# A second MoE with its last weight splits inside an expert's own first matmul and two narrower tiles, and an attention whose natural rows and one routing step are placed elsewhere

## Chip, core, metric

One core of a Trainium2 chip. The metric is the device time of one execution in microseconds; lower is better. The core has five engines that the text names: TensorE (PE in the profile, PEld for its weight loads), VectorE (DVE), ScalarE (ACT), GpSimd (POOL) and SyncE (SP, which here only issues DMAs).

## What is computed

Three stages run one after the other on 1536 tokens (2 batches of 768) of width 512 (8 heads of 64).

```python
# attention: a query sees the keys of its own cluster only
q_assign = argmax(q_n @ c_n.T); k_assign = argmax(k_n @ c_n.T)      # 16 clusters per head
scores = where(q_assign == k_assign, q @ k.T / 8, -1e9)
x = softmax(scores) @ v                                             # (1536, 512)
# first MoE: tokens with x @ w_skip > 0 go through one of 8 experts
x[sel] = x[sel] + gate * (relu(x[sel] @ w1[e]) @ w2[e])             # w1: 512x1024, w2: 1024x512
# second MoE, capacity 384 per expert
out = gate * (relu(x @ w1b[e]) @ w2b[e])                            # 0 for tokens over capacity
```

## The kernel before

**Attention.** Heads are worked in pairs g = 0 to 7. A hand-written schedule places calls at units u; a pair takes 12 units (2 heads x 6 key blocks). In each unit a score tile (`score_mm`, L290) goes through the exponential on ScalarE (L298), is rounded (L299) and its remainder taken on GpSimd (L301), and three units later it multiplies v (`pv`). Between them stand the preparation of the pair three ahead (`prep_T` psT, `prep_as`, `prep_oh`, `prep_mk`, and `stack_q`, whose DMAs fill AA and BB), the row maxima (`mpass`, L272) and the end of the pair before: `fin_den` and `fin_nat(g, 0)`, `fin_nat(g, 1)`. `fin_nat` makes half of a pair's rows in token order with three matmuls into psN, scales them into `xn` on VectorE, adds the routing logits into `lg` (L372), and in its second half issues two DMAs that store `xn` to `xa` and `xb`. All these take one PSUM tile at a time from a pool of six (`ps_w`). The orders of TensorE, ScalarE, GpSimd and SP are as written; VectorE's is the planner's in this stage.

**Routing in attention.** `early(lg)` is a generator whose steps run as hooks at units u0 + i (u0 = 58). It routes the first batch's tokens and finds the two experts to start with; the step at u0 + 6 picks these two in turn (L750 to L760), with its short-lived values in a PSUM tile (`scratch`).

**The second MoE.** `run` ends in a loop over places t = 1 to 7, where the experts stand sorted by their count, `caps` being the tokens that each place holds: 128, 256, 320, 256, 256, 256, 256, 128. The loop is written out in the order that every engine follows, VectorE too. An expert's first matmul (`l1`, L1432 to L1434) has 8 rows f of 4 x 3 matmuls, each with 128 columns of weights and caps[t] columns of x; a PSUM tile (two of them) holds two rows, or one where caps[t] is 320. ScalarE (L1437) and VectorE (L1438) then make ReLU and its remainder: `hh` and `hl`, and for the columns past 256 `hA`. The second matmul (`l2`, L1122 to L1124) takes 24 matmuls of 512 columns for each 128 tokens. Both use three products of rounded parts, and so each 512 KB piece of weights is split once (`split`): cast on ScalarE (L1036), remainder on VectorE (L1037). Pieces 0 to 3 are of the first matrix, 4 to 7 of the second; nine pairs of buffers (`spl`) hold them. The last place (t = 7 = Z) runs its first matmul unsplit. `nsplit` splits pieces of the next expert: piece 0 after the first quarter of `l1`, pieces 1 to 4 after `l1`, pieces 5 to 7 after `l2`. The pieces land in two sets of buffers that alternate, so `load(n + 2, i)` waits until piece i of expert n has been split.

Of the kernel before, what the change touches and what calls it, by code (L numbers as in the profile page):

```python
# [14 lines left out]
ALU = mybir.AluOpType  # L15
AX = mybir.AxisListType
# [6 lines left out]
def attention(ctx, tc, q, k, v, centroids, wcat, lgacc, xa, xb, idw, hooks, bind):  # L23
# [4 lines left out]
    C = S // 128  # L28
    HP = H // 2
    NP = B * HP  # L30
# [347 lines left out]
    def at(u, fn, *a):  # L378
        sched.setdefault(u, []).append((fn, a))
# [29 lines left out]
    for g in range(NP):  # L409
        u = 2 * C * g  # L410
        if g > 1:
            at(u + -32, load, g)
            at(u + -32, load_V, g)
        if g == 0:
            at(-20, load_V, 0)
            at(-20, load_V, 1)
            for x in ((prep_T, 0, 0), (cen_T,), (prep_H, 0, 0), (prep_L, 0, 0), (prep_T, 0, 1), (prep_H, 0, 1), (prep_L, 0, 1),
                      (prep_T, 0, 2), (prep_H, 0, 2), (prep_as, 0, 0), (prep_as, 0, 1), (stack_q, 0, 0, 0), (stack_q, 0, 1, 0),
                      (next, su), (prep_oh, 0, ((0, 1),)), (prep_as, 0, 2), (warm, 5), (prep_mk0, 0), (prep_oh, 0, ((1, 2),)),
                      (prep_L, 0, 2), (warm, 4), (prep_mk0, 1), (warm, 1), (stack_q, 0, 0, 1), (stack_q, 0, 1, 1),  # L420
                      (prep_V, 0)):
                at(-20, *x)
        else:
            w = (-10, -7, -7) if g == 1 else [u + x for x in (-21, -20, -18)]
            for i in range(3):
                at(w[i], prep_T, g, i)
            if g == 1:
                for i, (l, h) in enumerate(zip((-6, -5, -3), (-6, -5, -4))):
                    at(h, prep_H, g, i)
                    at(l, prep_L, g, i)  # L430
            w = (-5, -4, -3) if g == 1 else [u + x for x in (-19, -17, -16)]
            for i in range(3):
                at(w[i], prep_as, g, i)
            w = -1 if g == 1 else u + -14
            at(w, prep_oh, g)
            w = 3 if g == 1 else u + -12
            at(w, prep_mk, g)
            for h in range(2):
                x = 1 if g == 1 else w + 0
                at(x, stack_q, g, h, 0)  # L440
                at(x, stack_q, g, h, 1)
                at(w, stack_mk, g, h)
        if g:
            at(u + -10 if g > 1 else -2, prep_V, g)
        at(u + 2 * C + -3, fin_w, g)
        at(u + 2 * C + 4, fin_den, g)
        at(u + 2 * C + 4, fin_nat, g, 0)
        at(u + 2 * C + 5, fin_nat, g, 1)
    for u in sorted(set(sched) | set(hooks)):
        with ExitStack() as man:  # L450
            if u < 7:
# [8 lines left out]
class Moe:  # L460
    def __init__(self, ctx, tc, xa, xb, out, w1a, w2a, w1b, w2b, wg2, ident, landA, J=12):
# [13 lines left out]
        con, E, C = self.con, self.E, self.C  # L475
# [24 lines left out]
        self.tri = tri  # L500
        self.thr = {}
        self.c0 = {1: 128, 2: 256}
        self.caps = [128, 256, 320] + [256] * (E - 4) + [128]
        self.slots = [(p, i) for i in range(3) for p in range(E) if self.caps[p] > 128 * i]
        self.nov = (N_TOK - 128) // 128
        for m in (1, 2):
# [185 lines left out]
    def early(self, lg):  # L692
        nc, V, sm, E, C = self.nc, self.nc.vector, self.at, self.E, self.C
# [6 lines left out]
        def scratch(*ns):  # L700
            ps, o, out = self.ps(), 0, []
            for n in ns:
                out.append(ps[:, o:o + n])
                o += n
            return out

        by = lambda t, e: t.rearrange("p (j e) -> p j e", e=e)
# [16 lines left out]
        g, r = scratch(C, C)  # L724
# [9 lines left out]
        key = sm.tile([128, E], F32, name="key")  # L734
# [8 lines left out]
        ab = sm.tile([128, 2, E], F32, name="ab")  # L743
        es = sm.tile([128, 2], F32, name="pes")
        lh = sm.tile([128, 2], F32, name="lohi")
        mk = sm.tile([128, 2, 2], F32, name="pmk")
        abp, t, esp = scratch(2 * E, E, 2)
        abp = by(abp, E)
        for i in range(2):
            V.tensor_reduce(out=mk[:, i, 0:1], in_=key, axis=AX.X, op=ALU.max)  # L750
            V.tensor_scalar(out=abp[:, i], in0=key, scalar1=mk[:, i, 0:1], scalar2=None, op0=ALU.is_equal)
            V.tensor_tensor(out=t, in0=abp[:, i], in1=self.w8[:, 0, :], op=ALU.mult)
            V.tensor_reduce(out=mk[:, i, 1:2], in_=t, axis=AX.X, op=ALU.add)
            V.tensor_scalar(out=esp[:, i:i + 1], in0=mk[:, i, 1:2], scalar1=-1.0, scalar2=float(E), op0=ALU.mult, op1=ALU.add)
            if i == 0:
                V.scalar_tensor_tensor(out=key, in0=abp[:, 0], scalar=-65536.0, in1=key, op0=ALU.mult, op1=ALU.add)
        V.tensor_reduce(out=lh[:, 0:1], in_=esp.unsqueeze(1), axis=AX.X, op=ALU.min)
        V.tensor_reduce(out=lh[:, 1:2], in_=esp.unsqueeze(1), axis=AX.X, op=ALU.max)
        V.tensor_copy(es, esp)
        V.tensor_copy(ab, abp)  # L760
        yield
        self.eA = self.expert(es[:, 0:1], "dA", sm)
        self.eB = self.expert(es[:, 1:2], "dB", sm)
# [14 lines left out]
        abp, iap, kp = scratch(2 * E, 2 * C, C)  # L778
        abp, iap = by(abp, E), by(iap, C)
# [27 lines left out]
        inf, t, S = self.ids(self.spread(R0, rhs0, C), 2, self.rt, "e")  # L807
# [222 lines left out]
    def split(self, t):  # L1030
        nc = self.nc
        shp = [128, self.F]
        h = self.spl.tile(shp, F32R, name="wh")
        l = self.spl.tile(shp, F32R, name="wl")
        src = t if len(t.shape) == 2 else t.rearrange("p f d -> p (f d)")
        nc.scalar.copy(h, src)  # L1036
        nc.vector.tensor_tensor(out=l, in0=src, in1=h.bitcast(F32), op=ALU.subtract)  # L1037
        return h, l
# [314 lines left out]
    def run(self, lg, cap):  # L1353
# [7 lines left out]
        def load(n, i, t=None):  # L1361
            if n >= N:
                return
            if n >= n1:
                p = n - n1
                if p > 1 and p not in r2n:
                    r2n[p] = self.reg(self.namei2[:, p:p + 1])
                w = self.load(2, r2n.get(p, p), n, i, t)
            else:
                if n not in rL:  # L1370
                    rL[n] = self.reg(self.namei[:, n - 2:n - 1])
                w = self.load(1, rL[n], n, i, t)
            L[n, i] = w
# [13 lines left out]
        def put_splits(n, t, ks, i0):  # L1387
            for i, k in enumerate(ks):
                at(*divmod(17 * t + k, 17), lambda i=i0 + i: split(n, i))
# [144 lines left out]
        at(T, 7, lambda: self.fin2(S[n1], psU))  # L1534
        at(T, 4, lambda: xts(1, 0))
        at(T, 7, lambda: xts(1, 1))
        put_splits(n1 + 1, n1 + 1, (1, 2, 4, 5, 8, 9, 11, 13), 0)
        psS = play(T, self.l1_steps(sS["xt"], L1, hh, None) + self.l2n_steps(hh, W2(n1)))
        loads(n1 + 2, 4, 8)()
        self.fin2(sS, psS)  # L1540
# [1 line left out]
        Z = E - 1  # L1542
        for t in range(1, E):
            n = n1 + t
            for i in range(4, 8):
                load(n + 2, i)

            def nsplit(*ii):
                for i in ii:
                    if t + 1 < Z or t + 1 == Z and i >= 4:  # L1550
                        split(n + 1, i)

            hh, hl = self.new_h(256)
            if self.caps[t] > 256:
                h3 = self.rt.tile([128, 2, 8, 64], F32R, name="hA")
                self.h3 = h3[:, 0], h3[:, 1]
            nxt = sub(t + 1) if t < Z else []
            for s in nxt:
                self.gather(2, s)
            for k in range(4 if t < Z else 2):  # L1560
                if t < Z:
                    l1(t, k, hh, hl)
                else:
                    self.l1_native(sub(t)[0]["xt"], [L[n, i] for i in range(4)], k, hh[:, :, 0:128], hl[:, :, 0:128])
                if k == 0:
                    nsplit(0)
            nsplit(1, 2, 3, 4)
            for i in range(4):
                load(n + 2, i)
            pre = [lambda i=i: xts(t + 1, i) for i in range(len(nxt))] if t + 1 < Z else \  # L1570
                [lambda: self.xt_native(nxt[0])] if nxt else []
            for i, s in enumerate(sub(t)):
                ps = self.ps2()
                w = width(t, i)
                W2 = [SP[n, j] for j in range(4, 8)]
                self.l2(hh, hl, W2, range(0, 4), ps, i, w)
                if pre and (i or len(pre) == 3):
                    pre.pop(0)()
                self.l2(hh, hl, W2, range(4, 8), ps, i, w)
                self.fin2(s, ps, w)  # L1580
                if pre and i == 0:
                    pre.pop(0)()
            nsplit(5, 6, 7)
        self.overflow(2, [L[N - 1, i] for i in range(8)])
@with_exitstack
def tile_kernel(ctx, tc, q, k, v, centroids, moe_w_skip, moe_w_gate, moe_w1, moe_w2,
# [6 lines left out]
    with tc.manual_schedule(engines={ET.PE, ET.SP, ET.Pool, ET.Activation}):  # L1593
# [37 lines left out]
        for _k, _v in ((3, [early]), (u0 + 17, [moe.startA, moe.gatherAB]), (u1 + -14, [moe.xtA]), (u1 - 18, [swap]), (u1 + 2, [lambda: moe.l1A(0)]), (u1 + 6, [lambda: moe.l1A(1)])):  # L1631
            hooks.setdefault(_k, []).extend(_v)
        er = moe.early(lg)
        for i in (0, 1, 2, 4, 6, 8, 9, 11, 12, 13, 15):
            hooks.setdefault(u0 + i, []).append(lambda: next(er))
        for i in range(8):
            hooks.setdefault(u0 + 18 + i, []).append(lambda i=i: moe.loadA(i))
# [39 lines left out]
```

## Time and profile before

| | |
|---|---|
| Median of 3 runs | 659.49 us (656.88 to 660.16) |
| The profiled execution | 660.25 us; its span, first to last instruction, 658.4 us |
| Mean granted TensorE clock | 0.991 |
| Busy: PE, PEld, DVE, ACT, POOL | 623.5, 536.0, 404.0, 370.6, 259.7 us |

Busy time is the union of an engine's instructions. Matmuls are pipelined, so the distance between the starts of two of them, not the duration of one, tells their pace. Attention fills the span to about 300 us, the first MoE to about 467, the second to the end.

### The profile page before, as it was taken

To read this page: it belongs to the slowest core of one execution; us is meant where nothing else is said; L and a number is where in the kernel's file an instruction comes from. 1 tells how busy PE (TensorE), PEld (TensorE's weight loads), DVE (VectorE), ACT (ScalarE), POOL (GpSimd) and SP (SyncE) were. 2 spreads that over 40 slices of the span, in tenths; PEclk is the share of its full clock that TensorE was granted. 3 is DMA by queue.
4 is the path that set the end of the run, shared out by engine and by line. 5 is a ranking of instruction groups with operands and counts; after the bars stand their busy time and mean duration, and the time that the engine had idled before them with its cause. 6 is when DMAs were issued, how large, how long until landed. Compare 5 with 4: busy or idle time off the path is not lost. (4 is left out here: it accounts for less than half of the span.)

```text
span 658.4 us, 11633 instructions
## 1 busy us (share of the span) xinstructions
PE 623.5 (95%) x4104; PEld 536.0 (81%) x4104; DVE 404.0 (61%) x1003; ACT 370.6 (56%) x624; POOL 259.7 (39%) x197
## 2 busy tenths in 40 slices
PE   7889999999998999999999999999999899999994
PEld 6668888888877887879588999888778879888983
DVE  5958676767678785515777676655855536547431
ACT  4777787878778688872243443421355336455340
POOL 7665767777756578830120111100131112312110
PEclk9999999999999999999999999999999899999998
DMA  7964848484844549451478788882196616457100
GB/s 225 217 135 108 193 94 187 98 187 102 184 106 97 121 97 318 177 144 50 127 260 325 274 324 297 290 303 97 53 369 258 256 64 253 170 203 271 40 19 18
DMA packets 77104, 117.02 MB, mean 178 GB/s; under 512 B 27313, under 2 KB 42673, under 8 KB 77040
## 3 DMA queue, kind: packets, MB, share of 16 engines
q1 hardware_dynamic: 72752, 103.98, 52.7%
q0 software_dynamic: 4288, 12.24, 5.4%
q8 instruction: 34, 0.56, 0.3%
q14 instruction: 30, 0.25, 0.1%
HBM read 83.45 MB, written 12.98 MB: 146 GB/s over the span
## 5 line engine op out<-in xcount | busy, mean ns | idle before, releaser
L301 POOL TENSOR_TENSOR Pl<-P,Ph 128x768 fp32r<-128x768 f32 x93 | 170.3, 1840 | 69.3 <-ACT Ph L299 32.2
L1037 DVE TENSOR_TENSOR wl<-l,wh 128x1024 fp32r<-128x1024 f32 x84 | 99.9, 1221 | 57.1 <-ACT wh L1036 57.1
L272 DVE TENSOR_REDUCE m<-psx 128x1 f32<-128x384 f32 x192 | 98.0, 550 | 33.8 <-PE psx L271 32.9
L290 PE MATMUL pss<-BB,AA 128*128 128x384 f32 (+1 forms) x384 | 88.4, 352 | 9.4 <-DVE lg L372 3.6
L298 ACT ACTIVATE P<-pss 128x384 f32<-128x384 f32 x192 | 83.8, 489 | 23.1 <-PE pss L290 18.6
L1036 ACT CAST wh<-l 128x1024 fp32r<-128x1024 f32 x84 | 84.4, 1045 | 0.0
L299 ACT CAST Ph<-P 128x768 fp32r<-128x768 f32 x96 | 80.1, 835 | 4.2 <-PE pso L318 1.2
L290 PEld LDWEIGHTS pss<-BB,AA 128*128 128x128 f32 (+1 forms) x384 | 65.8, 190 | 16.0 <-ACT P L298 4.2
L1059 PE MATMUL psl<-xt,l 128*128 128x128 f32 x640 | 78.0, 277 | 0.4 <-ACT xt L1210 0.4
L1059 PEld LDWEIGHTS psl<-xt,l 128*128 128x128 f32 x640 | 74.8, 192 | 1.7 <-ACT xt L1210 0.5
L1156 POOL DMA_INDIRECT out_dram<-y,vsi x15 | 15.1, 1005 | 134.5 <-ACT y L1155 115.3
L316 PE MATMUL pso<-Ph,VA 128*65 128x384 f32 x192 | 65.7, 342 | 0.7 <-ACT DN L333 0.7
L318 PE MATMUL pso<-Ph,VL 128*64 128x384 f32 x192 | 65.9, 343 | 0.0
L320 PE MATMUL pso<-Pl,VA 128*65 128x384 f32 x192 | 65.6, 342 | 0.2 <-DVE Pl L301 0.2
L1432 PE MATMUL psl<-xh,wh 128*128 128x256 f32 (+1 forms) x192 | 55.7, 290 | 4.5 <-DVE hA L1438 2.7
L271 PE MATMUL psx<-AA,BB 128*128 128x384 f32 x192 | 51.6, 352 | 4.0 <-DVE m L272 1.5
L1433 PE MATMUL psl<-xl,wh 128*128 128x256 f32 (+1 forms) x192 | 54.9, 286 | 0.0
L1434 PE MATMUL psl<-xh,wl 128*128 128x256 f32 (+1 forms) x192 | 54.8, 285 | 0.0
L1148 POOL DMA_INDIRECT xb<-x,fsi x8 | 8.1, 1016 | 102.6 <-DVE x L1147 88.1
L271 PEld LDWEIGHTS psx<-AA,BB 128*128 128x128 f32 x192 | 34.1, 189 | 11.3 <-ACT P L298 5.0
L1122 PE MATMUL psl<-wh,hh 128*128 128x512 f32 x104 | 41.9, 403 | 0.0
L1432 PEld LDWEIGHTS psl<-xh,wh 128*128 128x128 f32 x192 | 36.6, 191 | 5.8 <-issue 3.0
(408 smaller groups left out, 1175.0 us busy)
## 6 DMA issues: line engine op xcount, KB each, us to landing
l<-in_moe_w_dram SPq DMA_DIRECT2D x128, 512.0 KB, 5.3
AA<-qkH SPq DMA_DIRECT2D x14, 384.0 KB, 4.9
vn<-in_v_dram SPq DMA_DIRECT2D x8, 384.0 KB
BB<-qkL SPq DMA_DIRECT2D x16, 192.0 KB, 3.4
xa<-xn SPq DMA_DIRECT2D x8, 384.0 KB
xb<-xn SPq DMA_DIRECT2D x8, 384.0 KB, 5.0
AA<-qkL SPq DMA_DIRECT2D x31, 96.0 KB, 4.1
BB<-qkH SPq DMA_DIRECT2D x31, 96.0 KB, 3.6
```

What stands on the lines that cost most here:

```text
L271: nc.tensor.matmul(ps, BB[:, 0, qc * 128:(qc + 1) * 128], AA[:, 0, f * HF:(f + 1) * HF], start=True, stop=True)
L272: nc.vector.tensor_reduce(out=hs[h]["m2"][:, qc, f:f + 1], in_=ps, axis=AX.X, op=ALU.max)
L290: nc.tensor.matmul(ps, AA[0:K, t, kc * 128:(kc + 1) * 128], BB[0:K, t, sl], start=(t == 0), stop=(t == 1))
L298: nc.scalar.activation(out=P[:, f * HF:(f + 1) * HF], in_=ps, func=AF.Exp, scale=1.0 / 8.0)
L299: nc.scalar.copy(Ph, P)
L301: eng.tensor_tensor(out=Pl, in0=P, in1=Ph.bitcast(F32), op=ALU.subtract)
L316: nc.tensor.matmul(o[0:D + 1, :], va, Ph[:, sl], start=(kc == 0), stop=False)
L318: nc.tensor.matmul(o[0:D, :], vl, Ph[:, sl], start=False, stop=False)
L1036: nc.scalar.copy(h, src)
L1037: nc.vector.tensor_tensor(out=l, in0=src, in1=h.bitcast(F32), op=ALU.subtract)
L1059: nc.tensor.matmul(st[k][:, q, :], L1[c][:, f * 128:(f + 1) * 128], xt[:, c, :], start=(c == 0), stop=(c == 3))
L1432: nc.tensor.matmul(ps[:, q, :], wh[:, fs], xh[:, c, 0:W], start=(c == 0), stop=False)
```

## The change

In attention, `fin_nat(g, 0)` and `fin_nat(g, 1)` of all pairs but the last stand one and two units later. The routing step that picks two experts becomes two steps with a PSUM tile each, one per expert, and the steps behind it come one unit later (the sixth stands at u0 + 6, the new seventh at u0 + 7). In the second MoE, places 5 and 6 hold 224 and 192 tokens instead of 256. Pieces 5 to 7 of an expert's weights are split inside its own `l1`, one after each of the first three quarters; pieces 0 to 4 of the next expert all follow `l1`; for the last place pieces 5 to 7 do too. Before the loop five pieces of the first expert are split instead of eight. `load(n + 2, 4..7)` moves from the loop's head to behind `load(n + 2, 0..3)`.

```diff
-        at(u + 2 * C + 4, fin_nat, g, 0)
-        at(u + 2 * C + 5, fin_nat, g, 1)
+        at(u + 2 * C + (5 if g < NP - 1 else 4), fin_nat, g, 0)
+        at(u + 2 * C + (7 if g < NP - 1 else 5), fin_nat, g, 1)
...
-        self.caps = [128, 256, 320] + [256] * (E - 4) + [128]
+        self.caps = [128, 256, 320] + [256] * (E - 6) + [224, 192, 128]
...
-        abp, t, esp = scratch(2 * E, E, 2)
-        abp = by(abp, E)
         for i in range(2):
+            abp, t, esp = scratch(E, E, 1)
             V.tensor_reduce(out=mk[:, i, 0:1], in_=key, axis=AX.X, op=ALU.max)
...
-        V.tensor_reduce(out=lh[:, 0:1], in_=esp.unsqueeze(1), axis=AX.X, op=ALU.min)
-        V.tensor_reduce(out=lh[:, 1:2], in_=esp.unsqueeze(1), axis=AX.X, op=ALU.max)
-        V.tensor_copy(es, esp)
-        V.tensor_copy(ab, abp)
+            V.tensor_copy(es[:, i:i + 1], esp)
+            V.tensor_copy(ab[:, i], abp)
+            if i == 0:
+                yield
+        V.tensor_reduce(out=lh[:, 0:1], in_=es.unsqueeze(1), axis=AX.X, op=ALU.min)
+        V.tensor_reduce(out=lh[:, 1:2], in_=es.unsqueeze(1), axis=AX.X, op=ALU.max)
...
-        put_splits(n1 + 1, n1 + 1, (1, 2, 4, 5, 8, 9, 11, 13), 0)
+        put_splits(n1 + 1, n1 + 1, (1, 2, 5, 9, 12), 0)
...
-            for i in range(4, 8):
-                load(n + 2, i)
...
-                if k == 0:
-                    nsplit(0)
-            nsplit(1, 2, 3, 4)
+                if t < Z and k < 3:
+                    split(n, 5 + k)
+            nsplit(0, 1, 2, 3, 4)
+            if t + 1 == Z:
+                nsplit(5, 6, 7)
             for i in range(4):
                 load(n + 2, i)
+            for i in range(4, 8):
+                load(n + 2, i)
...
-            nsplit(5, 6, 7)
...
-        for i in (0, 1, 2, 4, 6, 8, 9, 11, 12, 13, 15):
+        for i in (0, 1, 2, 4, 6, 7, 9, 10, 12, 13, 14, 16):
             hooks.setdefault(u0 + i, []).append(lambda: next(er))
```

## Rows read from the trace of the kernel before

**Rows 1.** The page, part 1: busy us, share of the span, instructions.

```profile
PE 623.5 (95%) x4104; PEld 536.0 (81%) x4104; DVE 404.0 (61%) x1003; ACT 370.6 (56%) x624; POOL 259.7 (39%) x197
```

**Rows 2.** Waits of PE over the span: us in total, times, longest.

```profile
PE pss L290 <- DVE lg L372: 3.6, 4, 1.2
...
PE psl L1432 <- DVE hA L1438: 2.7, 1, 2.7
PE psl L1432 <- DVE hl L1438: 1.7, 4, 0.4
...
PE pss L290 <- DVE key L756: 1.2, 1, 1.2
...
PE pss L290 <- DVE ab L760: 0.9, 1, 0.9
```

**Rows 3.** Timeline, place t = 2: start, duration (us), engine, instruction, idle time before.

```profile
508.01 2.93 ACT L1036 CAST wh<-l 128x1024 fp32r<-128x1024 f32 x3
...
513.06 0.38 ACT L1437 ACTIVATE hh<-psl 128x256 fp32r<-128x256 f32 x1
...
509.08 3.50 DVE L1037 TENSOR_TENSOR wl<-l,wh 128x1024 fp32r<-128x1024 f32 x3 [3.64 <-ACT wh L1036]
512.49 0.42 DVE L1438 SCALAR_TENSOR_TENSOR hl<-psl,hh 128x256 fp32r<-128x256 f32 x1
...
514.19 0.23 DVE L1438 SCALAR_TENSOR_TENSOR hA<-psl,hA 128x64 fp32r<-128x64 f32 x1 [0.29 <-ACT hA L1437]
...
513.57 0.61 PE L1432 MATMUL psl<-xh,wh 128*128 128x320 f32 x1 [2.72 <-DVE hA L1438]
```

**Rows 4.** Windows at half clock: length, busy of PE to POOL, clock, DMA share, GB/s.

```profile
513.20:516.60 3.40, 3.03 (x11) 3.06 (x12) 2.10 (x4) 1.40 (x3) 0.26 (x1) 0.50 0.98 344
...
212.80:216.20 3.40, 3.40 (x14) 3.04 (x13) 2.50 (x6) 0.90 (x2) 1.82 (x1) 0.50 0.01 2
```

**Rows 5.** Timeline of PE where place t = 3 waits.

```profile
548.40 0.28 PE L1434 MATMUL psl<-xh,wl 128*128 128x256 f32 x1
549.11 0.39 PE L1432 MATMUL psl<-xh,wh 128*128 128x256 f32 x1 [0.43 <-DVE hl L1438]
```

**Rows 6.** The pace of matmuls: the chain that ended last, and timelines.

```profile
451.01 0.90 PE psq L1177 x8
...
599.97 0.28 PE L1432 MATMUL psl<-xh,wh 128*128 128x256 f32 x1
...
601.67 0.28 PE L1432 MATMUL psl<-xh,wh 128*128 128x256 f32 x1
...
480.32 0.19 PEld L1128 LDWEIGHTS psl<-l,hh 128*128 128x128 f32 x1 [0.24 <-issue]
...
482.46 0.19 PEld L1128 LDWEIGHTS psl<-l,hh 128*128 128x128 f32 x1 [0.24 <-issue]
```

**Rows 7.** One group by form from 480 us: busy, mean ns of one.

```profile
L1438 DVE SCALAR_TENSOR_TENSOR hl<-psl,hh 128x512 fp32r<-128x512 f32 x20 | 13.8, 689 | 22.7 <-ACT hh L1437 22.1 <-issue 0.6
```

**Rows 8.** Timeline of ACT, place t = 2, two rows f one after the other.

```profile
518.73 0.38 ACT L1437 ACTIVATE hh<-psl 128x256 fp32r<-128x256 f32 x1 [0.66 <-PE psl L1434]
...
520.51 0.38 ACT L1437 ACTIVATE hh<-psl 128x256 fp32r<-128x256 f32 x1 [0.68 <-PE psl L1434]
```

**Rows 9.** Timeline of DVE, second matmul of place t = 5.

```profile
603.78 4.63 DVE L1037 TENSOR_TENSOR wl<-l,wh 128x1024 fp32r<-128x1024 f32 x4 [0.24 <-ACT wh L1036]
...
611.96 0.69 DVE L1420 TENSOR_TENSOR xl<-psxT,xh 128x512 fp32r<-128x512 f32 x1 [2.32 <-ACT xh L1419]
```

**Rows 10.** Timeline of PE and ACT, end of the second pair in attention.

```profile
101.31 0.60 PE L147 MATMUL psT<-idw,qkn 128*128 128x128 f32 x4
...
107.26 0.58 ACT L149 CAST qkH<-psT 128x512 fp32r<-128x512 f32 x1 [2.15 <-DMA BB<-qkH]
107.75 0.88 ACT L298 ACTIVATE P<-pss 128x384 f32<-128x384 f32 x2
...
108.99 0.59 PE L290 MATMUL pss<-BB,AA 128*128 128x384 f32 x2 [1.17 <-DVE lg L372]
```

More of the change, by code (lines that the diff above doesn't have):

```diff
@@ L746, in early @@
         mk = sm.tile([128, 2, 2], F32, name="pmk")
-        abp, t, esp = scratch(2 * E, E, 2)
-        abp = by(abp, E)
         for i in range(2):
+            abp, t, esp = scratch(E, E, 1)
             V.tensor_reduce(out=mk[:, i, 0:1], in_=key, axis=AX.X, op=ALU.max)
-            V.tensor_scalar(out=abp[:, i], in0=key, scalar1=mk[:, i, 0:1], scalar2=None, op0=ALU.is_equal)
-            V.tensor_tensor(out=t, in0=abp[:, i], in1=self.w8[:, 0, :], op=ALU.mult)
+            V.tensor_scalar(out=abp, in0=key, scalar1=mk[:, i, 0:1], scalar2=None, op0=ALU.is_equal)
+            V.tensor_tensor(out=t, in0=abp, in1=self.w8[:, 0, :], op=ALU.mult)
             V.tensor_reduce(out=mk[:, i, 1:2], in_=t, axis=AX.X, op=ALU.add)
-            V.tensor_scalar(out=esp[:, i:i + 1], in0=mk[:, i, 1:2], scalar1=-1.0, scalar2=float(E), op0=ALU.mult, op1=ALU.add)
+            V.tensor_scalar(out=esp, in0=mk[:, i, 1:2], scalar1=-1.0, scalar2=float(E), op0=ALU.mult, op1=ALU.add)
             if i == 0:
-                V.scalar_tensor_tensor(out=key, in0=abp[:, 0], scalar=-65536.0, in1=key, op0=ALU.mult, op1=ALU.add)
-        V.tensor_reduce(out=lh[:, 0:1], in_=esp.unsqueeze(1), axis=AX.X, op=ALU.min)
-        V.tensor_reduce(out=lh[:, 1:2], in_=esp.unsqueeze(1), axis=AX.X, op=ALU.max)
-        V.tensor_copy(es, esp)
-        V.tensor_copy(ab, abp)
+                V.scalar_tensor_tensor(out=key, in0=abp, scalar=-65536.0, in1=key, op0=ALU.mult, op1=ALU.add)
+            V.tensor_copy(es[:, i:i + 1], esp)
[4 more added lines that the diff above has]
+        V.tensor_reduce(out=lh[:, 1:2], in_=es.unsqueeze(1), axis=AX.X, op=ALU.max)
         yield
```

## Prediction

> **What bounds the kernel now.** I read the page's busy shares first, then the list of what TensorE waited for, then the timeline at each of those waits, then the stretches in which the clock was half. TensorE is busy for 95% of the span [rows 1], and no other engine comes near. So a change pays in two ways only: it takes work off TensorE, or it takes away a wait of TensorE. The list of its waits [rows 2] is short. Those that this change can touch are five entries: in attention `lg` L372 (3.6 us in 4 waits), `key` L756 (1.2) and `ab` L760 (0.9); in the second MoE `hA` L1438 (2.7, one wait) and `hl` L1438 (1.7 in 4). Together they are 10.1 us. Two of them are followed by a stretch in which the granted clock is 0.50, that is 1.2 GHz in place of 2.4 [rows 4]: one just after the `hA` wait, one just after the `key` and `ab` waits. In each the engine had stood idle before the clock fell.
>
> **The second MoE: the splits.** An expert's weights come in eight pieces; each is cast on ScalarE (L1036) and subtracted on VectorE (L1037), about 1.0 and 1.2 us each (three casts take 2.93, three subtractions 3.50 [rows 3]). Today pieces 5 to 7 of the next expert stand behind the whole second matmul of this one. Both engines then reach them at the moment the next expert's first matmul starts, ahead of its first ReLU. At t = 2 one sees the result [rows 3]: casts from 508.01, subtractions from 509.08 to 512.58, only then the first `hl` at 512.49; TensorE has filled its two PSUM tiles and starts again at 513.57, after 2.72 us of idle time. I count 2.7. The clock is half from 513.2 to 516.6, with 3.03 us of matmul in it [rows 4]; at full clock that is half as long: 1.5. At t = 3 to 6 the tiles are two rows of 256 wide and hold longer, so the same three splits cost less: 548.40 to 549.11 instead of 0.11, 0.6 each, four times [rows 2, 5]: 2.4.
>
> After the change each of these three splits follows a ReLU of its own expert's first matmul. With a 256-wide tile one step of k is 24 matmuls at 0.1133 us (599.97 to 601.67 holds 15 of them [rows 6]), 2.72 us. In it VectorE, the slower of the two, has 0.69 + 1.2 us to do [rows 3, 7], so the waits go entirely. At t = 2 the tile is 320 wide with one row per PSUM tile, and the chain hh, hl, hA, hA of one row lasts 513.06 to 514.42, 1.36 us [rows 3], against a row's matmuls of 1.78 [rows 8]. A cast after every second row sends a subtraction of 1.2 us between two `hl`. Followed row by row (row 1 done at 3.56 us, cast from 4.6, subtraction 5.7 to 6.9, `hl` of row 2 at 6.9, its chain done at 7.85, and TensorE wants that tile at 7.1), this costs 0.75 the first time, 0.35 the second, nothing the third: 1.1 of new waiting. Bounds: 0.6 if the subtraction slips behind `hl`, and 2.6 if the idle time brings the half clock with it (its 1.5).
>
> Behind the first matmul stand five splits now where four stood. Their subtractions run from 603.78 to 608.41 [rows 9]; a fifth ends at 609.6, and the first copy of the next expert's x, which stands behind them, at 610.3. The second copy comes at 611.96, after 2.32 us in which VectorE waited for its input; it does not move. I count nothing; if that cover were gone, each expert would start up to 1.2 later.
>
> The loads move with them: `load(n + 2, 4..7)` now waits for splits in the expert's own first matmul, while `load(n + 2, 0..3)`, put ahead of it in SP's queue, waits for splits already done. Nothing else stands behind them on that queue but the next expert's loads. Eight pieces of 512 KB are 4.2 MB, 12 us at the 344 GB/s of [rows 4], and they are due a whole expert later, at least 19 us (a first matmul of 4 x 2.72 and the 8.2 between the two rows of [rows 9]). I cost them at nothing; if a landing were late, the first split would be.
>
> **The second MoE: tiles of 224 and 192.** The experts in places 5 and 6 go from 256 columns to 224 and 192 in the first matmul, 96 matmuls each. No row of before has a split matmul narrower than 256. The nearest from below: eight matmuls with only 8 columns take 0.90 us, 0.1125 each [rows 6]. Their weights are 128 columns of fp32, as here; so the weight load sets this pace, and a 256-column matmul at 0.1133 already runs at it. Narrowing saves 192 x 0.0008 = 0.2 us. If the time followed the columns, it would be 96 x (0.0142 + 0.0283) = 4.1. From above: the plain fp32 matmul takes 480.32 to 482.46 for five of 512 columns, 0.428 us or 0.84 ns a column [rows 6]; at that pace 224 and 192 columns take 0.188 and 0.161, 11.7 us more in all. I take the weight-load row, since it has the same weights and the same neighbours. The second matmul keeps its 512 moving columns and its count; fewer output rows change nothing. The Trainium skill, "TensorE: Matmul & The Clock Gate", section "Back-to-back issue gap", would have a gap of N/2.4 + 2.5 ns, an estimate of 95.8 and 82.5 ns here, and a gain of 4.6 us. Its section "LDWEIGHTS (loading the stationary operand)" says that a load takes its columns over 1.2 GHz, 107 ns for 128, which speaks against a gain; the 8-column row agrees with the second, not the first.
>
> By the inputs that the reference draws, the experts in places 2 to 7 hold 266, 248, 244, 186, 156 and 125 tokens, so no smaller tile overflows.
>
> **Attention.** A pair's natural rows hold a PSUM tile (psN) from their matmuls to the last `lg` add. At 108.99 [rows 10] the second half of a score tile waits 1.17 us for one. ScalarE is the reason that tiles are short there: it stood 2.15 us for the landing of BB<-qkH, so the psT tile filled at 101.31 is still held then, and the scores ahead of it on ScalarE go only at 107.75. Without psN the score goes on at 107.6, but the next matmul wants the tile that the exponentials of 107.75 free at 108.25, the one after that the second, at 108.6. So half of the wait comes back: 1.8 of 3.6 us over the four pairs (0 if other allocations wait as long, 3.6 if none does). At one and two units later psN meets fewer copies of psT. The fifth pair falls on the routing step that the change halves: 1.2 + 0.9 us [rows 2] and 3.40 us at half clock [rows 4], worth 1.7. I take 1.2 of the waits, and the clock 6 times in 10, 1.0. Six later routing steps come one unit later; the one with eight small VectorE instructions now meets `prep_oh` of the last pair, for which I put 0.5 lost (0 to 1.2, the longest such wait). The two small copies more hide in VectorE's idle time (404 of 658 us busy, [rows 1]). The two 384 KB stores of a pair move with it on SP's queue, two units later; the next issue there is five units behind, or a weight load for the stage after attention. The gather after the last routing step still stands a unit behind it on POOL.
>
> **Sum.** MoE: 2.7 + 1.5 + 2.4 - 1.1 + 0.2 = 5.7. Attention: 1.8 + 1.2 + 1.0 - 0.5 = 3.5. The profiled execution took 660.25 us: 660.25 - 9.2 = 651.0. Its 660.25 lies 0.8 above the median of the runs, 659.49, and inside their spread, so I leave the sum as it is.
>
> **Rivals.** (a) Attention gives nothing: the tile is short because ScalarE waits for a DMA, so another allocation waits in psN's place, and the routing costs 0.5. 660.25 - 5.7 + 0.5 = 655.0. For it: the 2.15 us wait; against: the pairs after the fifth have the same psN with no psT beside it, and no wait. (b) The width pays: 651.0 + 0.2 - 4.1 = 647.1. Against it the 8-column row. (c) On the other side, narrow split matmuls fall to the pace of plain fp32: 651.0 + 0.2 + 11.7 = 662.9, slower than before. Everything else gained, 9.0 us, is eaten once the 192 matmuls take 47 ns more each, 160 ns. For it: no row narrower than 256 exists; against: nothing in the rows ties the pace to a width. (d) The routing and the rows, moved, wait as before in other places: no gain in attention and one wait of 0.85 for each of six moved steps, 660.25 - 5.7 + 5.1 = 659.6.
>
> **Chances.** The forecast 0.56, (a) 0.20, (b) 0.07, (c) 0.06, (d) 0.11. A difference under 0.5% of the median (656.2 to 662.8) can hardly be told from none. Faster: the forecast, (a), (b) and 0.02 of (d), 0.85; same 0.09; slower 0.06. The range begins where all waits go without residue (6.8 and 7.3 us gained: 646) and ends where attention gives nothing and the half clock stays at t = 2 (655.0 + 1.5 = 656.5). It leaves out (c) and most of (d).
>
> **What would show it.** After: no `hA` or `hl` wait over 0.3 us at t = 3 to 6; one or two of 0.3 to 0.8 inside t = 2; full clock around it; matmuls of 224 and 192 columns 0.110 to 0.114 us apart; `lg` waits under 0.5 or gone; half clock at 213 gone or shorter. I am wrong if the narrow ones are 0.16 apart, if the copies of x start the first matmul late, or if VectorE's new order in attention brings waits on `m` or on `oh`.

## The result and the profile after

The changed kernel takes 648.11 us (median of 4 runs, 647.92 to 648.88), against 659.2 us for the kernel before beside it (4 runs, 656.88 to 660.16). The ratio is 0.9839, with a 95% interval of 0.9812 to 0.9866. The profiled execution took 648.15 us with a span of 646.4, so 12.1 us less than that of before, where 9.2 were forecast.

The page of the kernel after, parts 1 and 2, answers to [rows 1]; the last line is the granted TensorE clock in 40 slices, in tenths:

```profile
PE 621.3 (96%) x4104; PEld 531.3 (82%) x4104; DVE 402.5 (62%) x1005; ACT 369.4 (57%) x624; POOL 258.3 (40%) x199
...
PEclk8999999999999999999999999999999999999998
```

TensorE has the same 4104 matmuls and is busy for 2.2 us less. The span shrank by 12.0, so nearly 10 us of idle time went. The list of what TensorE waited for, kernel after, answers to [rows 2]:

```profile
PE pss L290 <- ACT P L298: 2.4, 3, 1.0
...
PE psx L271 <- ACT P L298: 1.4, 3, 0.7
...
PE psl L1433 <- DVE hA L1439: 0.8, 1, 0.8
...
PE pss L290 <- DVE ab L757: 0.5, 1, 0.5
```

`lg` (3.6 us), `key` (1.2) and `hl` (1.7) are gone from it; `hA` went from 2.7 to 0.8 and `ab` from 0.9 to 0.5. One small line has grown: `psx`, the scores for the row maxima, waits 1.4 us for exponentials, where it waited 0.9 before.

The timeline of place t = 2, kernel after, answers to [rows 3]: ScalarE, VectorE, then TensorE, with the idle time ahead of an instruction in brackets.

```profile
506.58 1.04 ACT L1037 CAST wh<-l 128x1024 fp32r<-128x1024 f32 x1
507.51 0.39 ACT L1438 ACTIVATE hh<-psl 128x256 fp32r<-128x256 f32 x1
...
509.24 0.23 ACT L1438 ACTIVATE hA<-psl 128x64 fp32r<-128x64 f32 x1 [1.34 <-DVE hl L1439]
...
507.65 1.23 DVE L1038 TENSOR_TENSOR wl<-l,wh 128x1024 fp32r<-128x1024 f32 x1 [0.71 <-ACT wh L1037]
508.79 0.42 DVE L1439 SCALAR_TENSOR_TENSOR hl<-psl,hh 128x256 fp32r<-128x256 f32 x1
...
508.78 0.30 PE L1435 MATMUL psl<-xh,wl 128*128 128x320 f32 x1
509.87 0.39 PE L1433 MATMUL psl<-xh,wh 128*128 128x320 f32 x1 [0.79 <-DVE hA L1439]
```

One subtraction stands between two `hl` instead of three ahead of the first. It still delays the next one: ScalarE's `hh` of this row was done at 507.90, `hl` starts at 508.79, and TensorE stands 0.79 us instead of 2.72. The windows around this wait and at the place of the two half-clock stretches of [rows 4] (same columns), kernel after:

```profile
509.80:513.20 3.40, 3.33 (x23) 3.36 (x24) 2.18 (x4) 1.73 (x4) 0.00 (x0) 1.00 0.48 154
...
212.80:216.20 3.40, 3.40 (x24) 3.08 (x24) 2.90 (x9) 2.24 (x5) 1.97 (x2) 1.00 0.00 0
```

Both run at the full 2.4 GHz now, with 23 and 24 matmuls in a length that held 11 and 14. At t = 3, where the engine waited at [rows 5], the same two matmuls now follow each other at the usual distance, kernel after:

```profile
539.99 0.28 PE L1435 MATMUL psl<-xh,wl 128*128 128x256 f32 x1
540.10 0.28 PE L1433 MATMUL psl<-xh,wh 128*128 128x256 f32 x1
```

**Where the 12.1 us went**, by the starts of the same matmuls in the two profiles:

| stretch | before | after | gain | forecast |
|---|---|---|---|---|
| start of the span to first `pv` | 33.2 | 32.4 | 0.9 | 0 |
| attention, first to last `pv` | 259.8 | 255.4 | 4.4 | 3.5 |
| last `pv` to last `l1` of the first MoE | 183.3 | 183.3 | 0.0 | 0 |
| from there to the end | 182.1 | 175.4 | 6.7 | 5.7 |

Attention's ends are read from the group of the last product of `pv`, first line before, second line after (duration min/median/max in ns, then first and last start):

```profile
L320 PE MATMUL pso<-Pl,VA x192: 331/338/522, 33.2 to 293.0; 128*65 128x384 f32 x192
```

```profile
L320 PE MATMUL pso<-Pl,VA x192: 331/338/386, 32.4 to 287.8; 128*65 128x384 f32 x192
```

The 0.9 at the start cannot be put down to the change: that stretch is 33.2 to 34.6 us long in the three profiles with the attention of before and 32.2 to 34.3 in the five with that of after.

### The profile page after: what moved, and what is told of

It reads as the page before. It is cut to its first block, busy times and chain, and to the rows that moved or that the text cites. A ratio compares the mean times of both kernels' runs of the same rounds, so it can differ in the third digit from the quotient of the medians.

```text
span 646.4 us, 11643 instructions
## 1 busy us (share of the span) xinstructions
PE 621.3 (96%) x4104; PEld 531.3 (82%) x4104; DVE 402.5 (62%) x1005; ACT 369.4 (57%) x624; POOL 258.3 (40%) x199
## 5 line engine op out<-in xcount | busy, mean ns | idle before, releaser
L1157 POOL DMA_INDIRECT out_dram<-y,vsi x15 | 18.2, 1211 | 130.6 <-ACT y L1156 81.8
L271 PE MATMUL psx<-AA,BB 128*128 128x384 f32 x192 | 54.0, 359 | 4.7 <-DVE m L272 1.4
L1433 PE MATMUL psl<-xh,wh 128*128 128x256 f32 (+3 forms) x192 | 54.4, 283 | 0.8 <-DVE hA L1439 0.8
L1434 PE MATMUL psl<-xl,wh 128*128 128x256 f32 (+3 forms) x192 | 54.2, 282 | 0.0
L1435 PE MATMUL psl<-xh,wl 128*128 128x256 f32 (+3 forms) x192 | 54.1, 282 | 0.0
L1439 DVE SCALAR_TENSOR_TENSOR hl<-psl,hh 128x512 fp32r<-128x512 f32 (+3 forms) x28 | 16.4, 586 | 41.4 <-ACT hh L1438 41.3
L1123 PE MATMUL psl<-wh,hh 128*128 128x512 f32 (+2 forms) x104 | 41.8, 402 | 0.0
```

What stands on the lines that cost most here:

```text
L271: nc.tensor.matmul(ps, BB[:, 0, qc * 128:(qc + 1) * 128], AA[:, 0, f * HF:(f + 1) * HF], start=True, stop=True)
```

## Experiments

A kernel's time stands beside runs of the kernel before on the same chip; intervals are 95%. The half changes come first, then the width, then two disputed causes.

**The MoE's half alone.** The kernel after, with the tile widths and all of attention as before.

```diff
-        at(u + 2 * C + (5 if g < NP - 1 else 4), fin_nat, g, 0)
-        at(u + 2 * C + (7 if g < NP - 1 else 5), fin_nat, g, 1)
+        at(u + 2 * C + 4, fin_nat, g, 0)
+        at(u + 2 * C + 5, fin_nat, g, 1)
...
-        self.caps = [128, 256, 320] + [256] * (E - 6) + [224, 192, 128]
+        self.caps = [128, 256, 320] + [256] * (E - 4) + [128]
... (the routing step in one again, with its list of units)
```

> Only the splits and loads of the second MoE are changed; tile sizes and attention as before. Theory (the splits stood ahead of the ReLU): the wait of 2.7 us at t = 2 shrinks to about 0.8, the four of 0.4 to 0.5 vanish, no half clock near it: 6.0 to 6.6 us less than the kernel before, about 653. In attention the four waits on lg and those on key and ab stay. Rival (the gain after came from attention or from the narrower tiles): under 3 us.

Measured: 652.67 us, ratio 0.9911 (0.9882 to 0.994), about 5.9 us faster. The waits of TensorE in this kernel:

```profile
PE pss L290 <- DVE lg L372: 3.6, 4, 1.2
...
PE pss L290 <- DVE key L756: 1.2, 1, 1.2
...
PE pss L290 <- DVE ab L760: 0.9, 1, 0.9
PE psl L1432 <- DVE hA L1438: 0.8, 1, 0.8
```

The attention entries are those of [rows 2] to the tenth; the MoE's are those of after. The stretch from the last first-MoE `l1` to the end is 175.3 us, against 175.4 after and 182.1 before. So this gain comes from where the splits, and the loads with them, stand. The narrower tiles of the whole change do not show in the comparison: they gain 0.4 (below), but t = 1 took 11.39 us in the profile of after and 11.00 here, with the same instructions.

**Attention's half alone.** The kernel before with both attention edits.

```diff
-        at(u + 2 * C + 4, fin_nat, g, 0)
-        at(u + 2 * C + 5, fin_nat, g, 1)
+        at(u + 2 * C + (5 if g < NP - 1 else 4), fin_nat, g, 0)
+        at(u + 2 * C + (7 if g < NP - 1 else 5), fin_nat, g, 1)
... (and the routing step in two, as in the change)
```

> Only attention is changed, natural rows later and the routing step in two; second MoE as before. Theory: the lg waits (3.6 us) vanish but for 0.3, key and ab (2.0) fall to about 0.6, the half clock near 213 us goes (1.7 us of work): 4 to 6 us less, about 654. The 2.7 us wait of t = 2 and its half clock stay. Rival (the tile is short because ScalarE waits for a DMA, so another allocation waits): under 1 us less.

Measured: 655.54 us, ratio 0.9955 (0.9934 to 0.9977), about 3.0 us faster, less than expected. `lg` is gone from its waits, the MoE's two stay:

```profile
PE psl L1433 <- DVE hA L1439: 2.7, 1, 2.7
PE psl L1433 <- DVE hl L1439: 1.7, 4, 0.4
...
PE pss L290 <- DVE ab L757: 0.5, 1, 0.5
```

The two halves give 5.9 and 3.0; together 8.9, against 659.2 x (1 - 0.9839) = 10.6 for the whole. By the intervals of the ratios each carries 1.5 to 2 us of doubt, so the halves add up within what is measured.

**The natural rows alone.** The kernel before with the first two lines of that diff only.

> Only the natural rows stand later; routing and second MoE as before. Theory (psN held a sixth PSUM tile at the worst moment): the four lg waits go, 3.3 to 3.6 us less. At the fifth pair the routing step, still whole, meets psT alone: the waits on key and ab fall to about 1.2 together, and the half clock near 213 may go or stay (1.7). 4 to 6 us less in all. Rival (rows and routing only help together): under 2 us less.

Measured: 659.04 us, ratio 1.0013 (0.9995 to 1.0032): no gain. Its waits:

```profile
PE pss L290 <- ACT P L298: 2.9, 3, 1.3
PE psl L1432 <- DVE hA L1438: 2.7, 1, 2.7
...
PE pss L290 <- DVE ab L760: 1.8, 1, 1.8
...
PE psx L271 <- ACT P L298: 0.4, 2, 0.2
```

The 3.6 us of `lg` are gone, and the time is not. The two routing waits (`key` 1.2, then `ab` 0.9) are now a single one of 1.8, and the half clock comes behind it as before (this kernel's window just after the wait):

```profile
210.60:214.00 3.40, 3.23 (x10) 2.67 (x11) 3.34 (x10) 1.88 (x4) 2.05 (x2) 0.50 0.00 0
```

In the pairs without routing, 24 `pv` take 32.95, 33.16 and 32.91 us here against 33.13, 33.45 and 33.11 in the kernel before, so 0.67 us came back where about 2.8 us of `lg` waits went (three of the four).

**The routing step alone.** The kernel before with the step in two and the later units of the steps behind it.

```diff
-        abp, t, esp = scratch(2 * E, E, 2)
         for i in range(2):
+            abp, t, esp = scratch(E, E, 1)
...
+            if i == 0:
+                yield
...
-        for i in (0, 1, 2, 4, 6, 8, 9, 11, 12, 13, 15):
+        for i in (0, 1, 2, 4, 6, 7, 9, 10, 12, 13, 14, 16):
```

> Only the routing step is two steps, with the steps behind it one unit later; natural rows and second MoE as before. Theory: the four lg waits stay as they were; key and ab (2.0 us) fall to about 1.0, and the half clock near 213 goes if no longer idle stands before it: 1 to 2.7 us less. Rival (the step's place is of no account, only psN's): no change, key and ab waits of 2 us in all and the half clock stay.

Measured: 655.95 us, ratio 0.9966 (0.9948 to 0.9985), about 2.2 us faster. Where `key` and `ab` stood there is one wait:

```profile
PE pss L290 <- DVE lg L372: 3.6, 4, 1.2
PE pss L290 <- DVE pes L756: 1.2, 1, 1.2
```

There is no half clock near 213. The pair with this routing takes 34.2 us; before it took 37.4 with the half clock, and 35.8 in the MoE's half, which has the same attention and no half clock there. So about 1.6 us is the step's own gain, and 1.6 the clock's, in those executions of before that have it. VectorE's order in attention is the planner's and changes with every attention edit here; no run holds it fixed, so how much of this gain is the order's is open.

**The widths alone**, on the kernel before.

```diff
-        self.caps = [128, 256, 320] + [256] * (E - 4) + [128]
+        self.caps = [128, 256, 320] + [256] * (E - 6) + [224, 192, 128]
```

> Only the places 5 and 6 hold 224 and 192 tokens; the rest as before. Theory (the weight load of 128 columns sets the pace below 256 columns): matmuls 0.110 to 0.112 us apart, 0.2 to 0.6 us less in all, not to be told from no change. Rival 1 (pace follows the columns): 4.1 us less. Rival 2 (narrow ones at the pace of plain fp32): 11.7 us more.

Measured: 659.16 us, ratio 1.001 (0.9991 to 1.003): nothing. **The widths taken back**, on the kernel after:

```diff
-        self.caps = [128, 256, 320] + [256] * (E - 6) + [224, 192, 128]
+        self.caps = [128, 256, 320] + [256] * (E - 4) + [128]
```

> The changed kernel with places 5 and 6 back at 256 tokens. Theory (the weight load sets the pace below 256 columns): the two first matmuls take 10.9 us in place of 10.7 each, 0.4 us more in all, no difference that can be told. Rival (narrower tiles pay): 4.1 us more, 652.

Measured: 649.41 us, ratio 0.9843 (0.9804 to 0.9882), the same as after. The two first matmuls last 10.90 us each here and 10.71 and 10.70 in the kernel after, 0.2 us each. The pace itself, in the kernel after: the first product at the ends of a stretch of 15 matmuls, at 224 and at 192 columns.

```profile
582.88 0.28 PE L1433 MATMUL psl<-xh,wh 128*128 128x224 f32 x1
...
584.56 0.27 PE L1433 MATMUL psl<-xh,wh 128*128 128x224 f32 x1
...
605.88 0.28 PE L1433 MATMUL psl<-xh,wh 128*128 128x192 f32 x1
...
607.55 0.28 PE L1433 MATMUL psl<-xh,wh 128*128 128x192 f32 x1
```

1.68/15 is 0.112 and 1.67/15 is 0.111 us, against 0.1133 at 256 [rows 6].

**Widths to the token counts.** The kernel after with 272 for 320 columns at t = 2, and 192 and 160 at t = 5 and 6; the counts of the experts that stand there (266, 186, 156) fit.

```diff
-        self.caps = [128, 256, 320] + [256] * (E - 6) + [224, 192, 128]
+        self.caps = [128, 256, 272] + [256] * (E - 6) + [192, 160, 128]
```

> The changed kernel with places 2, 5 and 6 at 272, 192 and 160 tokens in place of 320, 224 and 192. Theory (columns set the pace above 256, the weight load below): place 2 goes from 0.1475 to about 0.125 us a matmul, 96 of them, 2.1 us less; places 5 and 6 stay at 0.110 to 0.112; its wait after the second row of t = 2 grows by up to 0.5, since a row is over sooner. 1.6 to 2.1 us less than the changed kernel, 646 to 646.5. Rival (the pace follows the columns everywhere): 4.9 us less. Rival (a floor above 272 columns as well): no gain.

Measured: 649.69 us, ratio 0.9857 (0.9829 to 0.9885), no faster than after. The same ends of 15 matmuls at 272 and at 160 columns:

```profile
507.81 0.29 PE L1433 MATMUL psl<-xh,wh 128*128 128x272 f32 x1
...
509.70 0.29 PE L1433 MATMUL psl<-xh,wh 128*128 128x272 f32 x1
...
605.84 0.27 PE L1433 MATMUL psl<-xh,wh 128*128 128x160 f32 x1
...
607.51 0.27 PE L1433 MATMUL psl<-xh,wh 128*128 128x160 f32 x1
```

Above 256 columns the two widths measured follow the columns: 1.89/15 is 0.126 us at 272, and 1.78/12 is 0.148 at 320 [rows 8], both 0.463 ns a column. This first matmul lasts 14.16 us instead of 15.37. Below, 160 columns go at 1.67/15, the same 0.111 as 192. The 1.2 us gained at 272 did not reach the end: the 256-wide first matmuls at t = 3 and 4 ran 0.118 apart here, 11.32 us each, and 0.1136 in the kernel after, 10.91 each. Why is open (see the last section). The stretch from the last first-MoE `l1` to the end took 175.1 us against 175.4; what comes ahead of the second MoE, which this edit leaves as it was, was some 2 us longer in this profile.

**No splits at all.** The kernel after, in which the experts of places 1 to 7 use plain fp32 matmuls on the landed weights (place 7's first matmul did already): one product in place of three rounded ones, and no cast or subtraction. Nothing of the computation is left out.

```diff
-                        nc.tensor.matmul(ps[:, q, :], wh[:, fs], xh[:, c, 0:W], start=(c == 0), stop=False)
-                        nc.tensor.matmul(ps[:, q, :], wh[:, fs], xl[:, c, 0:W], start=False, stop=False)
-                        nc.tensor.matmul(ps[:, q, :], wl[:, fs], xh[:, c, 0:W], start=False, stop=(c == 3))
+                        nc.tensor.matmul(ps[:, q, :], L[n1 + t, c][:, fs], X[t][:, c, 0:W], start=(c == 0), stop=(c == 3))
... (the second matmul likewise; every split and remainder gone)
```

> The changed kernel with the second MoE's experts at places 1 to 7 multiplied in plain fp32 straight from the landed weights: no splits, one matmul in place of three. By the pace of the plain fp32 rows (0.84 ns a column, 0.215 us for 256 and 0.428 for 512) a 256-token expert takes 32 x 0.215 + 16 x 0.428 = 13.7 us in place of 22.8; over all places 60 us less for TensorE. An expert's 4.2 MB then come every 13 us, 320 GB/s, near the most that the profile showed over 16 us (330): expected 590 to 605 us, bound in part by the loads. Rival (loads do not keep up, or the clock falls in the waits): 610 to 640. Rival (three rounded products are cheaper, as the kernel is written): over 648.

Measured: 679.35 us, ratio 1.0345 (1.0305 to 1.0386), slower. I had expected far less time, because I had misread what one plain matmul is in the trace. Two timeline lines of TensorE, and a window of 20 us, of this kernel:

```profile
531.73 3.60 PE L1560 MATMUL psl<-l,hh 128*128 128x512 f32 x8
535.16 0.60 PE L1048 MATMUL psxT<-idw,xg 128*128 128x128 f32 x4
```

```profile
520.00:540.00 20.00, 20.00 (x60) 10.09 (x59) 1.38 (x2) 2.87 (x8) 1.02 (x1) 1.00 0.34 118
```

Eight instructions take 535.16 - 531.73 = 3.43 us, 0.429 each. The group of this line's matmuls from `hh` has 208 instructions, while the program has 104 of them (13 blocks of up to 128 tokens times 8 rows f; `hA` is a group of its own): each is two instructions, 0.86 us for 512 columns. Three rounded products take the distance of the first two lines here, kernel after:

```profile
545.54 0.39 PE L1123 MATMUL psl<-wh,hh 128*128 128x512 f32 x1
...
546.23 0.39 PE L1123 MATMUL psl<-wh,hh 128*128 128x512 f32 x1
```

0.69 us. So splitting is cheaper on TensorE, and TensorE is the bound: it is busy for all 20.00 us of the window.

**Why score tiles were short: the DMA.** At [rows 10] ScalarE stands 2.15 us for BB<-qkH. SyncE issues that DMA, and its queue stood behind mask DMAs that wait for exponentials; its waits in the kernel before:

```profile
SPq L260 <- ACT P L298: 63.7, 6, 12.0
```

The theory: with both heads' `stack_q` ahead of the `stack_mk` in that queue, the wait of ScalarE goes, and the tile is free in time. On the kernel before and on the kernel after:

```diff
             for h in range(2):
                 ...
                 at(x, stack_q, g, h, 1)
+            for h in range(2):
                 at(w, stack_mk, g, h)
```

> The kernel before with one change in attention: both heads' stacking DMAs that read qkH and qkL stand ahead of both heads' mask DMAs on SP's queue (SP stands some 10 us at the first mask DMA with the second head's seven stacking DMAs behind it). Theory (PSUM tiles are short because ScalarE waits 2.2 us for these DMAs to read qkH): that wait goes, the four lg waits go with it, a pair takes 32.4 to 32.8 us in place of 33.1, and the fifth pair waits less on key and ab: 2 to 5 us less than the kernel before. Rival (psN holds the tile that is short, whatever ScalarE does): the lg waits and 33.1 us stay, no difference.

> The changed kernel with the same reordering of the stacking and mask DMAs. Theory (the later natural rows only moved the wait from lg to the psx and psT tiles, since ScalarE's wait is the cause): a pair goes from 32.95 to 32.4 to 32.7 us; with six such pairs 1.5 to 3 us less than the changed kernel, 645 to 646.6. Rival (32.95 is TensorE's own work): no difference.

Measured on the kernel before: 659.11 us, ratio 1.0001 (0.9979 to 1.0023). On the kernel after: 656.31 us, ratio 0.9943 (0.992 to 0.9966), which is some 7 us slower than after without it (ratio 0.9839; with the widths taken back, on the same chip as this run, 649.41 us). In the first, ScalarE's wait and the `lg` waits are gone, and the pair is no shorter, 33.45 us. VectorE's order in this stage is the planner's, and it came out another way: VectorE now stands at its own copy of the transposed q (VectorE, then ScalarE, kernel before with this edit).

```profile
105.82 0.69 DVE L150 COPY qkT<-psT 128x512 f32<-128x512 f32 x1 [4.23 <-ACT qkH L149]
...
105.21 0.58 ACT L149 CAST qkH<-psT 128x512 fp32r<-128x512 f32 x1
```

For 4.23 us it frees no tile, and TensorE has new waits for exponentials:

```profile
PE psL L342 <- ACT P L298: 2.6, 5, 0.5
```

In the second the pairs without routing take 33.9 us instead of 33.0, and its profile has half clock from 42 to 49 us and from 216 to 220, where that of after is at full clock. The theory is not borne out. But the edit also changed VectorE's order, so it did not test the DMA alone.

## Why the prediction was right, and where its sizes were off

**Bound.** Right: TensorE stayed the bound at 96%, and the gain is its idle time and its half clock. Of the 12.1 us, 0.9 lies in the start-up, within its scatter.

**Splits at t = 2.** Right in mechanism and size. The term was 2.7 + 1.5 - 1.1 = 3.1, and the first matmul went from 18.45 to 15.37 us, 3.1. Two new waits were forecast, 0.75 and 0.35, and both came. The first is the 0.79 of the list (1.0 by the starts of the matmuls, with the slower one after it). The second is too short for the list; the starts show it, kernel after:

```profile
513.32 0.31 PE L1435 MATMUL psl<-xh,wl 128*128 128x320 f32 x1
513.65 0.38 PE L1433 MATMUL psl<-xh,wh 128*128 128x320 f32 x1
```

That is 0.33 where 0.148 is usual, and 0.22 to the matmul after, together 0.25 us too much. The clock stayed full. That the half clock belongs to the 2.72 us of idle time rests on more than one pair: it follows at t = 2 in all six profiles with the old order of splits (the kernel before, and on it the widths, attention's half, the rows, the routing and the DMAs reordered) and in none of the five with the new order. In two of the six (the routing alone, and the DMAs reordered) it lasts 6.8 us instead of 3.4 and the first matmul takes 19.8 us, so 1.5 is the clock's price in the profile of before and not a fixed one.

**Splits at t = 3 to 6.** Right, but too small. I had 0.6 each, 2.4 in all, from one spacing at t = 3. In the run with the MoE's half alone the four first matmuls went from 11.61, 11.82, 11.63 and 11.62 to 10.90, 10.91, 10.90 and 10.91: 0.7 to 0.9 each, 3.1 in all. The term was taken from the gap at the wait alone; the distance to the next matmul is 0.22 there instead of 0.11, which the count left out, and t = 4 also ran at a slower pace before.

**Tiles of 224 and 192.** Right: the 8-column row decided. 0.111 and 0.112 us lie in the forecast's 0.110 to 0.114, and the gain is 0.2 each, 0.4 where 0.2 was forecast. Rival (b) fell: 160 columns are no faster than 192. The Trainium skill, "TensorE: Matmul & The Clock Gate", section "LDWEIGHTS (loading the stationary operand)", gives 128 columns over 1.2 GHz, 107 ns; the runs agree to within 5 ns, with 0.111 at 160 and 192 columns. Its section "Back-to-back issue gap", which the prediction drew on, gives N/2.4 + 2.5 for an isolated matmul and says that it under-counts at small N; here its 95.8 and 82.5 ns stand against 112 and 111.

**Rival (c)** fell too, and its price was wrong: I took 0.84 ns a column from single instructions at [rows 6], which are half a matmul each. By the run without splits it is 0.86 us for 512 columns, 1.68 ns a column, 0.376 and 0.323 us for 224 and 192. Against the 0.1133 it would have cost 96 x (0.263 + 0.210) = 45 us, not 11.7. The chance was small either way, but the bound was not one. The 8-column row of [rows 6] is eight instructions of four matmuls too; each of the eight has its own weight load, so it still gave the pace of a load.

**The natural rows.** This is the step that failed: "half of the wait comes back", 1.8 us. Counted by 24 `pv`, the four stretches with an `lg` wait (at 75.5, 109.0, 142.1 and 175.2 us) took 33.13, 33.45, 33.11 and 35.35 us before and take 32.95, 33.19, 32.93 and 35.16, so 0.8 less in all, under half of what was forecast; rival (a), under which nothing comes back, was about as near for this edit. The rest of the wait moved. The group of the row maxima's matmuls from 20 to 300 us, before and then after (busy, mean ns, then idle before them and its causes):

```profile
L271 PE MATMUL psx<-AA,BB 128*128 128x384 f32 x188 | 50.6, 352 | 3.2 <-DVE m L272 1.5 <-ACT P L298 0.9 <-DVE BB L279 0.4
```

```profile
L271 PE MATMUL psx<-AA,BB 128*128 128x384 f32 x185 | 52.5, 359 | 4.2 <-DVE m L272 1.4 <-ACT P L298 1.4 <-DVE BB L279 0.7
```

And the place itself, TensorE and ScalarE at the end of the second pair of after, which answers to [rows 10]:

```profile
104.93 0.66 PE L147 MATMUL psT<-idw,qkn 128*128 128x128 f32 x4
...
106.78 0.83 PE L271 MATMUL psx<-AA,BB 128*128 128x384 f32 x2 [0.26 <-ACT P L298]
...
105.75 0.59 ACT L149 CAST qkH<-psT 128x512 fp32r<-128x512 f32 x1 [1.64 <-DMA BB<-MK]
106.23 0.88 ACT L298 ACTIVATE P<-pss 128x384 f32<-128x384 f32 x2
```

ScalarE still stands 1.64 us for a DMA, and `psx` waits for the exponentials behind it. I summed the distances from each matmul's start to the next one's over the two pairs from the 25th to the 73rd `pv`: scores 20.39 to 18.77 us, row maxima 9.51 to 10.54, transposes 2.13 to 2.66, all together 66.58 to 66.15. Row maxima and transposes took 1.56 of the 1.62 us that the scores gave; the 0.4 that remains is at the natural rows' own matmuls, 3.29 to 2.86. That a tile is short because of ScalarE's wait was argued; the two DMA runs could not show it.

**The routing step.** Right that it pays, and too small. Waits, clock and the cost of moved steps were 1.2 + 1.0 - 0.5 = 1.7; the pair with it went from 37.40 to 34.27, 3.1. Some 1.6 of it is the clock (37.4 against 35.8 in runs with the same attention), which I had taken 6 times in 10, and 1.5 the step (1.0 to 1.5 over the five profiles with the attention of after, where this pair takes 34.3 to 34.8). The moved steps took nothing that shows: in this pair no wait for a value of theirs is in the list, so rival (d) fell. What is left stands at the first half of the step, 0.17 for `rden`, a value of `fin_den`, and 0.46 for `ab`; the second half, whose `ab` VectorE copies at 212.40, has none (TensorE, kernel after).

```profile
206.73 0.61 PE L290 MATMUL pss<-BB,AA 128*128 128x384 f32 x2 [0.17 <-DVE rden L344]
207.81 0.62 PE L290 MATMUL pss<-BB,AA 128*128 128x384 f32 x2 [0.46 <-DVE ab L757]
```

**The loads and the fifth split behind the first matmul** were costed at nothing, and the waits of after have no entry for either.

**Sum.** 651.0 - 648.15 is 2.85: 0.9 start-up, 1.0 from the second MoE, 0.9 from attention. There 1.4 too little for the routing stands against 1.0 too much for the rows, and some 0.4 came in stretches for which I had counted nothing (the seventh stretch of 24 `pv` is 0.19 shorter, the end of attention 0.3). So that attention's sum came near is in part luck: two errors of opposite sign, and a half clock that the profile of before happened to have.

## What to carry to other kernels

Work that must be done sometime on the engines that empty a matmul's tiles belongs one piece at a time behind each emptying, where a whole tile's matmuls cover it; put in one lump ahead of the first emptying it costs TensorE its length less the tiles in hand, and perhaps half the clock after that. A wait for a tile from a shared pool, taken away at one user, is only a gain if no other user takes the tile late as well: follow the chain two allocations on, and look for what makes the holder slow. Below the width at which the weight load sets the pace, a narrower tile gives next to nothing; and before a duration in the trace is called the price of an operation, count its instructions against the program's.

## What the hardware showed unexpectedly

A plain fp32 matmul of 512 columns is two TensorE instructions of 0.429 us; three products of rounded parts are three of 0.229 (546.23 - 545.54 = 0.69 in all). Three products are faster than one.

The 256-wide rounded matmuls ran at one of two paces, constant over most of a first matmul: 0.113 to 0.114 us apart, or 0.117 to 0.118. Which place gets which changed from profile to profile with the same instructions in that place: t = 1 has 0.118 in the kernels before and after and 0.114 in the MoE's half and with the widths taken back; t = 3 and 4 have 0.118 with the widths 272, 192 and 160, and 0.1136 after. A first matmul is 0.4 us longer at the slower pace. What sets it is open.

The half clock near 213 us came in the profile of before, in that of the natural rows alone and in the kernel after with the DMAs reordered, but not in the MoE's half nor with the widths alone, whose attention is that of before. The one at t = 2, behind 2.7 us of idle time, came in every profile with the old order of splits.
